# Waits that other waits imply are dropped, and transposed keys get three fixed buffers: a decode attention kernel on one core

## Chip, cores, metric

One core of one Trainium2 chip. The metric is the device time of one execution in microseconds, median of several; most executions agree within 0.1%. The profiler's span is some 1.7 us shorter than the timed execution.

## The reference, cut to what matters

```python
def _A_ref(x, k_cache, v_cache, wq, wo):        # B=4, Sq=1, D=1024, H=32, Sk=8192, Dh=128, bf16
    q = (x @ wq).reshape(B, Sq, H, Dh).transpose(0, 2, 1, 3)
    scores = jnp.einsum("bhqd,bhkd->bhqk", q, k_cache) * (Dh ** -0.5)
    p = _softmax(scores, axis=-1)
    o = jnp.einsum("bhqk,bhkd->bhqd", p, v_cache)
    return o.transpose(0, 2, 1, 3).reshape(B, Sq, H * Dh) @ wo
# ... b: a small gated MLP on the same x; result g*a + (1-g)*b, g = sigmoid of a dot product
```

Keys and values are 2 x 268 MB of the 575.69 MB that must be read. Everything else is small.

## The kernel before

The caches come in pairs of ring slots: four heads of keys (8.39 MB), then four heads of values, alternately. VectorE transposes each key pair in eight pieces of 128x2048 32-bit words, and TensorE multiplies each piece with a sliding window of the query. Values are multiplied as they land.

```python
    ttp = ctx.enter_context(tc.tile_pool(name="ttp", bufs=3))
    # ... manual order on TensorE, VectorE and GpSimd; waits come from the tracking of tiles
    nc.at_finalize(keep_weights)
    nc.at_finalize(begin_early)
    NS = 5
    ring = const.tile([P, NS, RING], BF, name="ring")      # 5 slots of 4.19 MB
    # ...
    def load_pair(src, n, apart=False):
        a = slots(2)
        if a + 1 < NS and not apart:
            nc.sync.dma_start(out=flat[:, lo:lo + 2 * n], in_=src)     # (lo = a * RING)
            return [flat[:, lo:lo + n], flat[:, lo + n:lo + 2 * n]]
        # ... a pair that wraps round the ring: two loads
    # ...
    def k_pair(d):
        # ...
        ks = load_pair(kv_view(A_k_cache, d), RING)
        for n in range(RD):                                # RD = 8
            kn, c = ks[n // JT], n % JT
            T = ttp.tile([P, CJ, 2, 32, 2], BF, name="T", tag="T")
            nc.vector.transpose(out=T[:].rearrange("p j h i e -> p (j h i e)").bitcast(U32),
                                in_=kn[:, c * CJ * Dh:(c + 1) * CJ * Dh].bitcast(U32))
            s = QP - 1 - (RD * t + n)
            for he in range(4):
                half, e = divmod(he, 2)
                for z in range(2):
                    nc.tensor.matmul(sps[:, z, :], lhsT=Z[:, he, s:s + P], rhs=T[:, 16 * z:16 * z + 16, half, :, e],
                                     start=(t == 0 and n == 0 and he == 0),
                                     stop=(t == GD - 1 and n == RD - 1 and he == 3))
```

## Time and profile before

| | before |
|---|---|
| time, median of 3 | 1345.83 us (1345.19 to 1346.19) |
| span in the profile | 1344.2 us, 7958 instructions, 418 of them only wait (EVENT_SEMAPHORE) |
| TensorE / VectorE busy | 77% / 46% |
| transfer queue 1 busy | 99.4% of 16 engines |
| fetches of instructions (queues 8 and 14) | 27 and 7 packets |

A semaphore is a counter by which one engine, or a load, tells another that something is done. In the built programs a transpose carries one wait itself; a further wait stands before it as an instruction of its own, an EVENT_SEMAPHORE. A load is issued when its instruction runs, and has landed when all its data are there. In the lines of profiles, PE is TensorE (PEld its loading of weights), DVE is VectorE, ACT is ScalarE, POOL is GpSimd and SP is SyncE; L375 is line 375 of that run's kernel, and x8 a count.

The end of the chain of work (start, duration, what): the last load of output weights lands at 1340.10, and only four matmuls and a copy follow it.

```profile
1325.25 14.85 DMA ring<-in_A_wo_dram
1340.10 0.04 issue
1340.14 1.04 PE acc L212 x4
...
1341.20 0.57 ACT res L522
```

### The profile page before, as it was taken

The page shows a single profiled execution, that of the slowest core. Times are in us where ns is not written, and L with a number is a line of the kernel's source. Part 1 is how long each engine was busy: PE and PEld are TensorE (multiplying, and loading weights), DVE is VectorE, ACT ScalarE, POOL GpSimd, SP SyncE. Part 2 cuts the span into 40 slices and gives each one's busy share as a digit, 9 for nine tenths or more (in the row PEclk, how much of TensorE's full clock was granted, in tenths as well). Part 3 has the DMA queues.
Part 4 walks back from the last instruction along what each step waited for, and adds up shares of the span by engine and source line. Part 5 has one row for each costly group of instructions (what it writes and reads, how often), then busy time and mean ns, then how long its engine had stood idle before and what let it go on. Part 6 is the DMA issues. An engine that isn't in the chain of part 4 may idle for free.

```text
span 1344.2 us, 7958 instructions
## 1 busy us (share of the span) xinstructions
PE 1034.7 (77%) x4536; PEld 226.7 (17%) x2348; DVE 611.8 (46%) x358; ACT 50.6 (4%) x46; POOL 55.4 (4%) x90
## 2 busy tenths in 40 slices
PE   2665877777788787778987779598778678876898
PEld 0111111111111121111211112111111112111221
DVE  1555655544345554336455556146555244556000
ACT  0000100001000010001000010000100010000100
POOL 2000010001000010001000010000100010000100
PEclk9787988988998888899888889898889799889799
DMA  9999999999999999999999999999999999999997
GB/s 414 437 430 429 440 428 428 444 433 418 446 430 426 432 435 432 438 429 432 430 435 433 437 435 424 431 430 435 433 425 441 431 426 442 431 424 427 434 424 313
DMA packets 14174, 576.19 MB, mean 429 GB/s; under 512 B 1582, under 2 KB 1590, under 8 KB 2108
## 3 DMA queue, kind: packets, MB, share of 16 engines
q1 hardware_dynamic: 14132, 575.69, 99.4%
q8 instruction: 27, 0.44, 0.1%
q14 instruction: 7, 0.06, 0.0%
q10 hardware_dynamic: 8, 0.00, 0.0%
HBM read 575.68 MB, written 0.01 MB: 428 GB/s over the span
## 4 chain that ended last, share of the span: by engine, by line
DMA 66%; PE 13%; DVE 11%; issue 9%; ACT 0%; another core or an unknown queue 0%; DVEq 0%; SPq 0%
DMA ring<-in_A_k_cache_dram 53%; PE o_ps L455 11%; DVE T L375 11%; DMA ring<-in_A_v_cache_dram 9%; DMA ring<-in_B_w_gate_dram 3%; PE S_ps L381 2%; DMA ring<-in_A_wo_dram 1%; ACT PB L426 0%; PE small L475 0%; PE acc L246 0%; DVEq L375 0%; ACT OS L467 0%; PE acc L212 0%; ACT res L522 0%
## 5 line engine op out<-in xcount | busy, mean ns | idle before, releaser
L375 DVE STREAM_TRANSPOSE T<-ring 128x2048 uint32<-128x2048 uint32 x256 | 566.6, 2277 | 494.9 <-DMA ring<-in_A_k_cache_dram 483.5
L381 PE MATMUL S_ps<-T,Z 128*128 128x512 bf16 x2048 | 520.2, 409 | 220.8 <-DVE T L375 220.3
L455 PE MATMUL o_ps<-ring,PB 128*32 128x512 bf16 x2048 | 462.2, 389 | 51.8 <-DMA ring<-in_A_v_cache_dram 47.2
L381 PEld LDWEIGHTS <-Z 128*128 128x128 bf16 x1024 | 105.8, 103 | 630.8 <-issue 623.6
L455 PEld LDWEIGHTS <-PB 128*32 128x32 bf16 x1024 | 101.0, 99 | 409.5 <-issue 368.3
L468 DVE SCALAR_TENSOR_TENSOR OS<-o_ps,mE,OS 128x512 f32<-128x512 f32 x8 | 6.0, 750 | 102.4 <-ACT OS L467 102.4
L406 ACT ACTIVATE PTs<-S_ps,negm 128x1024 bf16<-128x1024 f32 x8 | 8.9, 1114 | 965.3 <-DVE negm L403 965.2
L358 POOL TENSOR_TENSOR Z<-qa,mq 128x16 bf16<-128x16 bf16 x32 | 9.1, 286 | 744.7 <-PE S_ps L381 659.6
L428 POOL COPY PB<-PT 32x1024 bf16<-32x1024 bf16 x16 | 30.5, 1904 | 81.4 <-PE o_ps L455 81.0
L426 ACT COPY PB<-PT 32x1024 bf16<-32x1024 bf16 x16 | 30.6, 1911 | 1.5 <-DVE PT L408 1.4
L309 DVE CAST LT<-small 128x64 bf16<-128x64 f32 x2 | 0.5, 225 | 40.8 <-PE small L307 40.8
L159 PE MATMUL small<-identb,x 6*128 6x6 bf16 x8 | 0.6, 197 | 23.1 <-DMA x<-in_gate_w_dram 23.1
L399 POOL PARTITION_ALL_REDUCE gmx<-mex x8 | 3.2, 397 | 341.3 <-DVE mex L396 341.3
L394 DVE TENSOR_REDUCE m<-S_ps 128x1 f32<-128x1024 f32 x8 | 9.8, 1226 | 15.9 <-PE S_ps L381 15.9
L212 PE MATMUL acc<-ring,LT 128*4 128x512 bf16 x64 | 14.9, 378 | 1.9 <-DMA ring<-in_A_wo_dram 1.1
L408 DVE STREAM_TRANSPOSE PT<-PTs 128x1024 bf16<-128x1024 bf16 x8 | 10.0, 1246 | 12.1 <-ACT PTs L406 12.1
L212 PE MATMUL acc<-ring,hT 128*4 128x512 bf16 x56 | 12.2, 379 | 0.0
L467 ACT ACTIVATE OS<-o_ps,mE 128x512 f32<-128x512 f32 x8 | 5.5, 687 | 157.4 <-PE o_ps L455 157.4
L475 PEld LDWEIGHTS small<-selg,OS 128*128 128x128 f32 x64 | 9.0, 208 | 4.1 <-issue 3.9
L475 PE MATMUL small<-selg,OS 128*128 128x16 f32 x64 | 8.7, 269 | 0.0
L246 PE MATMUL o_ps<-ring,xw 128*4 128x512 bf16 x56 | 5.5, 519 | 3.5 <-DMA ring<-in_B_w_gate_dram 3.5
L246 PE MATMUL S_ps<-ring,xw 128*4 128x512 bf16 x64 | 6.4, 590 | 0.3 <-DVE xw L161 0.3
(71 smaller groups left out, 63.9 us busy)
## 6 DMA issues: line engine op xcount, KB each, us to landing
ring<-in_A_k_cache_dram SPq DMA_DIRECT2D x14, 4096.0 KB
ring<-in_A_v_cache_dram SPq DMA_DIRECT2D x14, 4096.0 KB, 31.3
ring<-in_B_w_gate_dram SPq DMA_DIRECT2D x1, 7168.0 KB, 37.9
ring<-in_B_w_up_dram SPq DMA_DIRECT2D x1, 7168.0 KB, 39.2
ring<-in_B_w_down_dram SPq DMA_DIRECT2D x2, 3584.0 KB, 27.8
ring<-in_A_wo_dram SPq DMA_DIRECT2D x6, 1024.0 KB, 21.0
ring<-in_A_v_cache_dram SPq DMA_DIRECT2D x2, 2048.0 KB, 25.7
ring<-in_A_v_cache_dram SPq DMA_DIRECT2D x4, 1024.0 KB, 24.6
```

Of the source, the lines that this page charges most:

```text
L212: nc.tensor.matmul(out_ap, lhsT=lhsT, rhs=rhs, start=start, stop=True, skip_group_check=True)
L246: nc.tensor.matmul(ps[32 * k:32 * k + Bn, z, :], lhsT=xT[TW * half + t], rhs=cols(w, t, 4 * z + k), start=(half + t == 0), stop=(half == 1 ...
L358: nc.gpsimd.tensor_tensor(out=Z[:, :, QP - 1:QP - 1 + P].rearrange("p e (q c) -> p e q c", c=QP)[:, :, :, 0], in0=qa[:, :, h0:h0 + NQ, b], ...
L375: nc.vector.transpose(out=T[:].rearrange("p j h i e -> p (j h i e)").bitcast(U32), in_=kn[:, c * CJ * Dh:(c + 1) * CJ * Dh].bitcast(U32))
L381: nc.tensor.matmul(sps[:, z, :], lhsT=Z[:, he, s:s + P], rhs=T[:, 16 * z:16 * z + 16, half, :, e], start=(t == 0 and n == 0 and he == 0), ...
L394: nc.vector.tensor_reduce(out=m1[:], in_=sps[:].rearrange("p z n -> p (z n)"), axis=AX.X, op=ALU.max)
L406: nc.scalar.activation(out=PTs[:], in_=sps[:].rearrange("p z n -> p (z n)"), func=ACT.Exp, bias=negm[:, 0:1], scale=scale, accum_out=rs[:, ...
L408: nc.vector.transpose(out=PT[:].rearrange("p j i -> p (j i)"), in_=PTs[:])
L426: nc.scalar.copy(out=Bv[at, :, :, q, :], in_=Pv[at])
L428: nc.gpsimd.tensor_copy(out=Bv[at, :, :, q, :], in_=Pv[at])
L455: nc.tensor.matmul(o_ps[row:row + NM, e, :], lhsT=PB[:, RD * t + c, z, w].rearrange("p e s j -> p (e s j)"), rhs=vn[:, j0 * Dh:(j0 + 4) * ...
L475: nc.tensor.matmul(oT[:, :], lhsT=o_sb[:, q * Dh:(q + 1) * Dh], rhs=selg[:, q].rearrange("p t s -> p (t s)"), start=(q == 0), stop=(q == 3))
```

## The change

When the program is finalised, all engines' instructions are replayed in an order that their semaphores allow. Each engine keeps a clock of what it knows from its waits; a wait is dropped if the engine, or the instruction's other waits, already imply it. The pool for transposed keys gives way to three constant buffers, used in turn. The intent is fewer semaphore instructions and no releases of pool tiles.

```diff
+def drop_implied(nc):
+    # ... streams: the instructions of each engine; known[e]: what engine e has seen
+                        keep = [w for w in waits if not seen(known[e], w)]
+                        for w in list(keep):
+                            k = dict(known[e])
+                            for o in keep:
+                                if o is not w:
+                                    learn(k, o)
+                            if seen(k, w):
+                                keep.remove(w)
+    # ... learn the waits, record the clock at each update, put in the instructions with fewer waits
-    ttp = ctx.enter_context(tc.tile_pool(name="ttp", bufs=3))
+    nc.at_finalize(drop_implied)
+    TB = [const.tile([P, CJ * P], BF, name=f"TB{i}") for i in range(3)]
+    tb_turn = [0]
+    def turned(rows, n, dtype=BF):
+        t = TB[tb_turn[0] % 3]
+        tb_turn[0] += 1
+        return t[0:rows, 0:n] if dtype == BF else t[0:rows, 0:2 * n].bitcast(dtype)
-            T = ttp.tile([P, CJ, 2, 32, 2], BF, name="T", tag="T")
-            nc.vector.transpose(out=T[:].rearrange("p j h i e -> p (j h i e)").bitcast(U32),
+            flat_t = turned(P, CJ * P)
+            T = flat_t.rearrange("p (j h i e) -> p j h i e", j=CJ, h=2, e=2)
+            nc.vector.transpose(out=flat_t.bitcast(U32),
# ... the other users of that pool (gate weights, queries, hidden values, output) take turned(...) as well
```

More of the change, by code (lines that the diff above doesn't have):

```diff
@@ L1 @@
+import copy
 from contextlib import ExitStack
@@ L36, in keep_weights, with seen, learn @@
             block.instructions = kept
+def drop_implied(nc):
+    for f in nc.m.functions:
+        for block in f.blocks[1:2]:
+            streams, at = {}, {}
+            for i in block.instructions:
+                streams.setdefault(i.engine, []).append(i)
+            known = {e: {} for e in streams}
+            level, reached = {}, {}
+            at = {e: 0 for e in streams}
+            def seen(k, w):
+                return k.get(w.id, 0) >= w.wait_value
+            def learn(k, w):
+                for v, clock in reached[w.id]:
+                    if v >= w.wait_value:
+                        for n, x in clock.items():
+                            k[n] = max(k.get(n, 0), x)
+                        break
+                k[w.id] = max(k.get(w.id, 0), w.wait_value)
+            moved, plan = True, []
+            while moved:
+                moved = False
+                for e, todo in streams.items():
+                    while at[e] < len(todo):
+                        i = todo[at[e]]
+                        y = i.sync_info
+                        waits = list(y.on_wait) if y is not None else []
+                        if any(w.wait_mode != "sem-ge-imm" or level.get(w.id, 0) < w.wait_value for w in waits):
+                            break
+                        keep = [w for w in waits if not seen(known[e], w)]
[6 more added lines that the diff above has]
+                                keep.remove(w)
+                        for w in waits:
+                            learn(known[e], w)
+                        if len(keep) < len(waits):
+                            plan.append((i, keep))
+                        for u in (y.on_update if y is not None else []):
+                            level[u.id] = level.get(u.id, 0) + u.update_value
+                            reached.setdefault(u.id, []).append((level[u.id], {**known[e], u.id: level[u.id]}))
+                        at[e] += 1
+                        moved = True
+            if all(at[e] == len(todo) for e, todo in streams.items()):
+                less = {i.name: copy.replace(i, sync_info=mybir.SyncInfo(on_wait=keep, on_update=list(i.sync_info.on_update)))
+                        for i, keep in plan}
+                block.instructions = [less.get(i.name, i) for i in block.instructions]
@@ L218, in gates @@
         rg_ps = small([P, 2, Bn])
-        wrep = ttp.tile([P, 2, DT, P], BF, name="wrep", tag="T")
+        wrep = turned(P, 2 * DT * P).rearrange("p (i t c) -> p i t c", i=2, t=DT)
         for i in range(2):
@@ L229, in add_x @@
     def add_x():
-        xf = ttp.tile([Bn, D], F32, name="xf", tag="T")
-        nc.vector.tensor_copy(out=xf[:], in_=x6[0:Bn])
+        xf = turned(Bn, D, F32)
+        nc.vector.tensor_copy(out=xf, in_=x6[0:Bn])
         for n in range(NH):
@@ L252, in q_done @@
     def q_done():
-        qs = ttp.tile([P, 2, 4, P], BF, name="qs", tag="T")
-        nc.vector.tensor_copy(out=qs[:].rearrange("p z c d -> p z (c d)"), in_=q_ps[:])
+        qs = turned(P, 8 * P).rearrange("p (z c d) -> p z c d", z=2, c=4)
+        nc.vector.tensor_copy(out=qs.rearrange("p z c d -> p z (c d)"), in_=q_ps[:])
         qt = small([P, 2, 4, 4, 32], BF)
@@ L276, in h_done @@
     def h_done():
-        h = ttp.tile([P, 2, 512], F32, name="h", tag="T")
-        nc.scalar.activation(out=h[:], in_=o_ps[:], func=ACT.Silu)
-        nc.vector.tensor_tensor(out=h[:], in0=h[:], in1=acc4[:], op=ALU.mult)
+        h = turned(P, 1024, F32).rearrange("p (z n) -> p z n", z=2)
+        nc.scalar.activation(out=h, in_=o_ps[:], func=ACT.Silu)
+        nc.vector.tensor_tensor(out=h, in0=h, in1=acc4[:], op=ALU.mult)
         for z in range(2):
@@ L518 @@
         use()
-    res = ttp.tile([Bn, D], BF, name="res", tag="T")
+    res = turned(Bn, D)
     nc.vector.tensor_copy(out=res[:, 0:NB], in_=acc[:, 0:NB])
```

## The prediction

> **What bounds the kernel now.** I read the page first, looking for whatever has no idle time. Each digit is a tenth of a slice of 33.6 us; the last row is what the transfer engines moved.
>
> ```profile
> span 1344.2 us, 7958 instructions
> ...
> PE   2665877777788787778987779598778678876898
> ...
> DVE  1555655544345554336455556146555244556000
> ...
> DMA  9999999999999999999999999999999999999997
> GB/s 414 437 430 429 440 428 428 444 433 418 446 430 426 432 435 432 438 429 432 430 435 433 437 435 424 431 430 435 433 425 441 431 426 442 431 424 427 434 424 313
> ...
> q1 hardware_dynamic: 14132, 575.69, 99.4%
> ```
>
> TensorE is busy 77% and VectorE 46%. The 16 DMA engines are busy 99.4% of the span, with no slice under nine tenths but the last. So the kernel is one long read of 575.69 MB. The second view is the table by stretches: middle, then the end in two.
>
> ```profile
> 60.00:1320.00 1260.00, 993.73 (x4258) 216.61 (x2175) 593.07 (x333) 47.91 (x42) 45.07 (x62) 0.90 1.00 432
> ...
> 1330.00:1340.00 10.00, 9.11 (x58) 2.44 (x40) 0.48 (x2) 0.00 (x0) 0.00 (x0) 1.00 0.60 242
> 1340.00:1344.20 4.20, 1.02 (x4) 0.08 (x1) 0.68 (x1) 0.57 (x1) 0.00 (x0) 0.97 0.01 2
> ```
>
> The last two columns are DMA share and GB/s. From 60 to 1320 us the share is 1.00 at 432 GB/s; only the last 14 us are not full. The third question is whether busy transfers hide a late issue, that is, how much work is queued when a load is issued. The chain of work shows one period:
>
> ```profile
> 529.02 2.28 DVE T L375
> ...
> 531.32 29.65 DMA ring<-in_A_k_cache_dram
> ...
> 561.00 0.05 DVEq L375
> ...
> 561.26 2.07 issue
> ...
> 567.72 2.28 DVE T L375
> ...
> 570.01 29.68 DMA ring<-in_A_k_cache_dram
> ```
>
> A key load is issued when the fourth transpose frees half a pair (531.32, 570.01) and lands 29.65 us later. A pair is 4 heads x 8192 x 128 x 2 bytes = 8.39 MB, so 19.4 us at 432 GB/s. The other 29.65 - 19.4 = 10.2 us it stands behind the value load issued before it. So this issue could come about 10 us later, or any amount earlier, and the engines would still not run dry. The chain's "DMA 66%, DVE 11%" looks like a loop through VectorE, but it counts the time in the queue as travel: the period, 570.01 - 531.32 = 38.7 us, is simply two pairs, 2 x 19.4 = 38.8 us of transfer.
>
> **What the Trainium skill says.** "DMA: Bandwidth & Descriptors", section "Where 436 GB/s comes from", gives 435.2 GB/s for the 16 ports into SBUF, and about 358 GB/s as the HBM limit of one core, which it says binds HBM loads. This trace disagrees with the second: 432 GB/s was measured, and the measurement decides. It agrees with the first, 0.7% under it. As an estimate from that page, 575.69 MB / 435.2 GB/s = 1322.8 us is the least that the bytes can take; 2% off the present time would be 0.98 x 1345.83 = 1318.9 us, below it. "Perfetto Trace Analysis", section "Identifying Dependency Chains", says that an instruction waiting on several engines may get EventSemaphore instructions in front of it for the further conditions. This trace agrees: the view of the transpose's line has nearly one for each of the 256 transposes. "VectorE: DVE Perf Modes", section "The DRAIN you can't avoid", reports that eight copies took the same time with a semaphore after each as with one after the last. That concerns increments, but it points the same way: the transposes here follow one another at 17.68 us / 8 = 2.21 us although one lasts 2.27 us, so the extra wait opens no gap.
>
> ```profile
> L375 DVE STREAM_TRANSPOSE T<-ring x256: 2253/2269/2315, 49.9 to 1229.7; 128x2048 uint32<-128x2048 uint32 x128
> L375 DVEq EVENT_SEMAPHORE  x252: 21/21/15795, 52.2 to 1225.4; - x126
> ```
>
> (21 ns is the median; the 15.8 us is time blocked in such a wait, not work.)
>
> **The change part by part.**
> 1. Transposed keys in three fixed buffers in place of a pool of three. Same size (8 KB a partition each), same order of use, same instructions. No byte of DMA and no operation is added. What goes is the pool's release of a buffer, which I take to be why nearly every transpose has a second wait. Cost or gain in work: zero.
> 2. Implied waits dropped. Most of the 252 waits before transposes should go: the transpose three earlier on the same engine is implied by the TensorE wait (those matmuls waited for it), and the landing of a pair is seen once. Also most of the 57 + 17 on the load lines of the SyncE queue, since "VectorE has read the slot" implies "its load has landed"; and a few tens elsewhere. Work removed: 252 x 21 ns = 5.3 us on VectorE's sequencer, beside transposes that keep the engine full, and about 74 x 17 to 28 ns = 1.3 to 2.1 us on SyncE's, which mostly waits. On the path that sets the end in the middle: 0, since an earlier issue only lengthens a queue already 10 us deep.
> 3. First transpose after a landing. It starts about 0.1 us after the data (561.00 to 561.10), 0.05 us of it the extra wait. Over 32 pairs that is 1.6 us at most, if it were on the path; with 10 us queued it is not. I count 0.
> 4. Head. The first load is issued at 0.00 us without waiting. Saving 0.
> 5. Tail. The last weights land at 1340.10, four matmuls take 1.04, the copy 0.57, then the output goes and the program closes at 1344.2. There are one 17 ns wait before the second store and seven of 17 to 28 ns on SyncE in the closing: at most 0.017 + 7 x 0.028 = 0.2 us, of which I count half, 0.1 us. The last weight load has an extra wait too (17 ns, at 1325.2), but is issued 14.85 us before it lands, behind other data.
> 6. Instruction fetch: 27 packets, 0.44 MB, 0.1% of the DMA time. About 350 fewer of 7958 instructions is 4% of 0.1%, some 0.06 us.
>
> Sum: 0.1 + 0.06 = about 0.2 us, inside the spread of the three runs before (1345.19 to 1346.19). I choose 1345.6.
>
> **The rivals.**
> - VectorE or TensorE sets the rhythm and the waits are on it. For it: the chain names the transposes for 11% and "issue" for 9%, and TensorE waits 220 us in total for transposes. The 1.6 us of step 3, plus perhaps 2 us on SyncE, would make 1342 to 1343 us. Against it: DMA share 1.00 over 1260 us. VectorE also waits 483.5 us for key loads; the engine that waits for the transfers does not limit them.
> - Loads issued earlier give the engines a fuller queue and a better rate. The most is 432 to 435.2 GB/s, 0.7%, so 1336 us. For it: the slices vary from 418 to 446. Against it: slices above 435 must be an artefact of how bytes are booked, and they alternate with low ones; the queue is never empty, so a deeper one shows the engines nothing new.
> - A new dependency takes the place of the pool's. Fixed buffers are ordered by overlap of regions, and the odd users (gate weights, queries, hidden values, the output) share them; a coarser order could make a transpose wait for a wrong reader. If a whole group of matmuls (15 us) were added to each of 32 key pairs, the 10 us queue would run dry by up to 5 us a pair: 160 us, about 1500 us. Against it: TensorE goes in order and the rotation is the same, so the last reader of a buffer is the same matmul. I give it 1%.
> - The order of issue on SyncE and ScalarE, which the program does not fix by hand, comes out otherwise. A changed order in the last 20 us could cost or save 1 to 3 us, since there the DMA share falls to 0.60. This widens the range.
>
> **Range and chances.** The spread of repeats is 1.0 us; tail order and chip add 1 to 2 us either way: 1343.0 to 1347.5. Faster by over 2% would beat the port estimate: 0.5%. Slower by over 2% needs a starved queue: 1%. Within 2%: 98.5%.
>
> **What would show it.** Right: DMA share 1.00 and 431 to 433 GB/s from 60 to 1320 us, key loads still landing about 30 us after issue, EVENT_SEMAPHORE at the transposes down from 252 to under 70, transposes still 2.27 us each, last weights landing at 1340 within 1 us. Step 2 wrong: the count stays near 252 (then the waits were not implied). Step 3 wrong, and the first rival right: the whole shortens by 1.5 us or more at the same GB/s. The whole wrong: a middle slice of the DMA row under nine tenths, or issue to landing near 19.4 us, an empty queue.

## More of the kernel before

The page's two queues for instructions, with packets, MB and share of 16 engines:

```profile
q8 instruction: 27, 0.44, 0.1%
q14 instruction: 7, 0.06, 0.0%
```

## The result, and the profile after

Ratios here are the mean time of one kernel's fast runs over the mean of the other's fast runs of the same rounds, so not quite the ratio of the medians quoted.

| | before | after |
|---|---|---|
| time, median | 1346.01 us (4 runs, 1345.19 to 1346.39) | 1344.20 us (4 runs, 1344.16 to 1344.51) |
| ratio | | 0.9988, 95% interval 0.9971 to 1.0005 |
| span | 1344.2 us | 1342.8 us |
| instructions that only wait | 418 (VectorE 259, SyncE 93, GpSimd 31) | 81 (34, 17, 15) |

(Where a text written beforehand says 82, it counts a clearing of semaphores on GpSimd, which is not a wait.)

The predicted 1345.6 us (1343.0 to 1347.5) holds. Yet the four runs of each kernel do not overlap, and 1.4 us of span is more than the 0.2 us of my sum. First the lines of the page after:

```profile
span 1342.8 us, 7621 instructions
...
DMA  9999999999999999999999999999999999999997
...
q1 hardware_dynamic: 14132, 575.69, 99.5%
q8 instruction: 27, 0.44, 0.1%
q14 instruction: 5, 0.04, 0.0%
```

337 instructions are gone and the transfer engines are as full as before. The table by stretches answers to the one of before: same share, same 432 GB/s from 60 to 1320 us.

```profile
60.00:1320.00 1260.00, 994.79 (x4267) 216.47 (x2178) 593.50 (x333) 46.57 (x41) 45.04 (x62) 0.89 1.00 432
1330.00:1340.00 10.00, 8.79 (x53) 1.77 (x33) 0.49 (x2) 0.05 (x1) 0.00 (x0) 1.00 0.58 236
```

The view of the transpose's line (durations in ns: least, median, most) shows 30 waits where 252 were, and no duration changed; the chain of work still has a key load of nearly 30 us, so the queue is as deep as before.

```profile
L443 DVE STREAM_TRANSPOSE TB<-ring x256: 2254/2270/2315, 49.7 to 1227.8; 128x2048 uint32<-128x2048 uint32 x128
L443 DVEq EVENT_SEMAPHORE  x30: 21/21/21, 59.4 to 1221.1; - x30
```

```profile
530.44 29.77 DMA ring<-in_A_k_cache_dram
...
560.30 17.67 DVE TB L443 x8
...
1323.81 15.04 DMA ring<-in_A_wo_dram
1338.85 0.04 issue
1338.89 1.04 PE acc L279 x4
...
1339.95 0.57 ACT TB L590
```

So where does 1.4 us come from? The closing, from the last landing to the end, shrank from 1344.2 - 1340.10 = 4.1 us to 1342.8 - 1338.85 = 3.95 us: 0.15 us. The other 1.25 us is the landing of the last weights, 1340.10 against 1338.85.

Adding up all transfer packets of the traces shows something odd: the bytes moved by any moment up to 1320 us agree within what 0.3 us moves. The transfers as a whole are not faster. But a load counts as landed when the last of the 16 engines has done its part, and these do not finish together: in the last 10 us of the kernel before their share falls to 0.60, and the trace of before ends with one engine alone on the last eight packets of 4 KB, until 1339.64. In the changed kernel the last packet ends at 1338.43.

What else uses these engines? The instructions. Queue 14 brings 8 KB packets, one whenever VectorE has run about 128 more instructions of 64 bytes: in the trace of before the VectorE count stands at 64, 193, 319, 448 and 577 at five of the seven; the remaining two go with other streams, by the counts GpSimd (66) and SyncE (79). After, VectorE's counts at a fetch are 59, 190 and 321: three in place of five. A 64 KB data packet takes 2.42 us, and the one next to a VectorE fetch takes 0.5 to 0.7 us longer. Two fetches fewer, 0.6 us each, would be 1.2 us on one engine. That is theory F (fetches): VectorE's fetched instructions cost one transfer engine time, and every load waits for the slowest engine. Theory A is that of the prediction: only the closing can shorten, the rest is chance. Theory W is that the waiting itself cost the time.

### The profile page after: what moved, and what is told of

Same layout as the page of the kernel before. It is cut to its first block, busy times and chain, and to the rows that moved or that the text cites. A ratio compares the mean times of both kernels' runs of the same rounds, so it can differ in the third digit from the quotient of the medians.

```text
span 1342.8 us, 7621 instructions
## 1 busy us (share of the span) xinstructions
PE 1033.8 (77%) x4536; PEld 226.1 (17%) x2348; DVE 612.4 (46%) x358; ACT 50.6 (4%) x46; POOL 55.3 (4%) x90
## 4 chain that ended last, share of the span: by engine, by line
DMA 65%; DVE 20%; PE 12%; another core or an unknown queue 1%; ACT 0%; issue 0%; SPq 0%; DVEq 0%
DMA ring<-in_A_k_cache_dram 56%; DVE TB L443 20%; PE o_ps L523 10%; DMA ring<-in_A_v_cache_dram 7%; DMA x<-in_gate_w_dram 2%; DMA ring<-in_A_wo_dram 1%; PE S_ps L449 1%; ACT PB L494 0%; PE S_ps L313 0%; PE acc L313 0%; PE small L543 0%; ACT OS L535 0%; PE acc L279 0%; DVE OS L536 0%
## 5 line engine op out<-in xcount | busy, mean ns | idle before, releaser
L443 DVE STREAM_TRANSPOSE TB<-ring 128x2048 uint32<-128x2048 uint32 x256 | 567.3, 2278 | 495.2 <-DMA ring<-in_A_k_cache_dram 493.9
L449 PE MATMUL S_ps<-TB,Z 128*128 128x512 bf16 x2048 | 520.0, 409 | 218.7 <-DVE TB L443 218.5
```

The lines of the kernel that those rows point to most:

```text
L443: nc.vector.transpose(out=flat_t.bitcast(U32), in_=kn[:, c * CJ * Dh:(c + 1) * CJ * Dh].bitcast(U32))
```

## The experiments

The first four separate the parts and give a control; the next four add instructions that wait for nothing; the last four test the queue that hides delays. Times are medians; "kernel before" is the median of nine runs on the same chip in the same rounds.

### The control, the change again, and each part alone

Edits: none; none; and, from the changed kernel and the kernel before:

```diff
# e3_fixed_only: from the changed kernel
-    nc.at_finalize(drop_implied)
# e4_drop_only: from the kernel before
+    nc.at_finalize(drop_implied)
```

> The kernel before, unchanged, timed against itself: the control for the 1.8 us between the medians (1346.01 and 1344.20). Theory A (transfers bound it, only the closing microseconds can shorten): ratio 1.000 within 0.0005, and a second profile whose landing times wander against the first by 0.5 to 1.5 us, as those of the changed kernel do. Rival B (the waits cost a real microsecond in the body): the control is tight, within 0.3 us of the first profile at the landing of the last weights (1340.10 us), so that the 1.25 us by which the changed kernel lands earlier is not chance.

> The changed kernel, unchanged. Theory A: 0.9995 to 0.9999 of the kernel before, that is 0.1 to 0.7 us less (about 0.15 us of the closing, the rest chance). Rival B: 0.9985 to 0.9991, that is 1.2 to 2 us less, with an interval that leaves 1 out.

> Fixed buffers for the transposed keys alone, no wait dropped. Theory A: equal to the kernel before within 0.3 us, and the extra wait instructions before the transposes fall from 252 to well under that, since I put the second wait down to the pool's release. Rival B, buffers: carries most of the 1.2 to 2 us. Rival C: the count stays near 252, because the second wait is a wait for the load or for the engine itself, and it is the dropping that removes it.

> Implied waits dropped, with the pool of three buffers kept. Theory A: equal to the changed kernel within 0.3 us; extra wait instructions in all about 80 as in the changed kernel (82), if implied waits include the pool's. Rival B, waits: carries the 1.2 to 2 us alone. If the pool's release hides the order from the dropping, the count stays well above 82.

Measured, kernel before 1346.09 us:

| run | time us (5 runs) | ratio, 95% interval | instructions that only wait | queue 14 packets | last weights landed |
|---|---|---|---|---|---|
| e1_before_again | 1345.58 (1345.12 to 1345.78) | 0.9997, 0.9984 to 1.0011 | 418 | 7 | 1339.94 |
| e3_fixed_only | 1345.68 (1345.22 to 1346.34) | 1.0000, 0.9987 to 1.0012 | 418 | 7 | 1339.41 |
| e2_after_again | 1344.26 (1344.03 to 1344.61) | 0.9989, 0.9976 to 1.0001 | 81 | 5 | 1338.88 |
| e4_drop_only | 1344.43 (1344.21 to 1344.49) | 0.9989, 0.9977 to 1.0002 | 81 | 5 | 1338.85 |

The rounds' intervals include 1, barely. But all 14 runs with dropped waits lie at 1344.03 to 1344.61, and the ten runs of the control and of the fixed buffers at 1345.12 and above; of the kernel before one run in nine lies lower (1344.74). About 1.3 us is real and belongs to the dropping alone. The landings say the same: 1339.41 to 1340.10 in the three profiles with all waits, 1338.85 to 1338.88 in the three without. Theory A as I wrote it falls: the rest is not chance. The fixed buffers do nothing, and they did not remove the second wait either. The view of the transpose's line in e3_fixed_only:

```profile
L442 DVEq EVENT_SEMAPHORE  x252: 21/21/15893, 52.1 to 1224.7; - x126
```

The built programs say why: nearly every transpose waits for TensorE and for VectorE's own semaphore, that is for the write of the same buffer three transposes earlier, whether the buffer is from a pool or fixed.

### Waits that never block: instructions without waiting

Edit, on top of the changed kernel: before every chosen instruction of one engine, a wait on the first semaphore value that this engine ever waited for.

```diff
+def pad(nc, engine, pick, k):
+    # ... held: the first wait of this engine; for each later instruction that pick() chooses:
+                        for _ in range(k):
+                            out.append(mybir.InstEventSemaphore(name=f"I-{900000 + n}", engine=engine, debug=i.debug, bass_nofuse=True,
+                                                                sync_info=mybir.SyncInfo(on_wait=[held], on_update=[])))
+    nc.at_finalize(lambda nc: pad(nc, mybir.EngineType.DVE, lambda i: isinstance(i, mybir.InstStreamTranspose), 1))
# e6: 4 in place of 1; e7: Pool, InstTensorTensor, 32; e8: PE, InstLdweights, 1
```

> The changed kernel with one wait put back before every stream transpose on VectorE, on a semaphore value that was reached at the very start, so that it never blocks: instructions without waiting. Theory F (fetching VectorE's instructions, 8 KB per 128 of them, takes about 0.6 us each from one of the 16 transfer engines, and every load waits for the slowest of these): VectorE has 264 instructions more, so the fetches in the body (queue 14) go from 5 back to 7, and the time from 1344.2 back to 1345.2 to 1345.8, last weights landing 1.0 to 1.4 us later than in the changed kernel. Rival W (it was the waiting): no blocking wait comes back, so 1344.2 within 0.3.

> Four such waits before every stream transpose on VectorE, 1056 in all. Theory F: 8 more fetches than in the changed kernel, so 8 x 0.6 = about 5 us more: 1347.5 to 1350.5. Rival W: 1344.2 within 0.3, as the transposes still fill VectorE (4 x 21 ns beside 2.2 us each).

> The changed kernel with 1024 waits that never block on GpSimd (32 before each of 32 small multiplications): GpSimd's instruction stream is fetched 8 times more. Theory F with one transfer engine for everybody's instructions: as with VectorE, about 5 us more. Theory F with a transfer engine of its own for each instruction stream: less than that, 0 to 3 us, until that engine becomes the slowest. Rival W: 1344.2 within 0.3.

> The changed kernel with 2271 waits that never block on TensorE, one before every weight load: its stream is fetched about 9 times more, 16 KB each. Theory F with TensorE's fetches on the slowest transfer engine: 9 x 0.5 us = 4 to 6 us more. Theory F with them on another: 0 to 3 us. Rival W: 1344.2 within 0.5 (51 ns each on TensorE's sequencer, about 70 per pair = 3.6 us of a 38.7 us period that has 9 us to spare).

Measured, kernel before 1345.59 us in these rounds; the changed kernel was 1344.26 in its own, on another chip, where the kernel before took 1346.09. So the differences below carry some 0.5 us of doubt:

| run | time us (5 runs) | against 1344.26 | packets on queues 14 / 8 | last weights landed |
|---|---|---|---|---|
| e5_pad_dve_264 | 1345.03 (1344.32 to 1345.43) | +0.8 | 7 / 27 | 1339.64 |
| e6_pad_dve_1056 | 1351.76 (1350.22 to 1352.98) | +7.5 | 13 / 27 | 1347.34 |
| e7_pad_pool_1024 | 1346.13 (1345.99 to 1346.19) | +1.9 | 13 / 27 | 1340.47 |
| e8_pad_pe_2048 | 1346.63 (1345.57 to 1347.12) | +2.4 | 5 / 35 | 1340.27 |

Theory W falls: nothing here blocks, and 1056 instructions on VectorE cost 7.5 us (6.2 us against the kernel before of the same rounds: ratio 1.0042, interval 1.0029 to 1.0056, clear of 1). I had expected 1350.5 at most. Do they delay the transposes instead? No. In e6_pad_dve_1056 eight transposes take what they took in the changed kernel (17.67 us in the chain above); the page and the table by stretches show the transfers suffering:

```profile
563.05 17.66 DVE L462 STREAM_TRANSPOSE TB<-ring 128x2048 uint32<-128x2048 uint32 x8 [21.10 <-DMA ring<-in_A_k_cache_dram]
```

```profile
q1 hardware_dynamic: 14132, 575.69, 99.0%
...
q14 instruction: 13, 0.11, 0.0%
```

```profile
60.00:800.00 740.00, 566.84 (x2427) 121.63 (x1235) 370.00 (x210) 29.79 (x26) 28.25 (x39) 0.89 1.00 432
800.00:1320.00 520.00, 416.59 (x1803) 92.73 (x925) 223.02 (x124) 16.79 (x15) 16.78 (x23) 0.90 1.00 428
```

The second stretch gives way (428 GB/s, against 431 in the changed kernel run again). I read this as: one engine falls behind step by step, the other 15 run ahead on what is queued, and when their lead has used up the queue they too lose time. The landing times of single engines, below, show the first half of that; the second half is argued.

The steps can be seen at single fetches. Take the landing times of e5_pad_dve_264 minus those of the changed kernel (e2_after_again), and the times of the fetches on queue 14:

| between the landings at | fetch in only one of them | difference before and after it |
|---|---|---|
| 337 and 346 us | e5 at 338.2 | +0.43 to +1.51 |
| 813 and 852 us | e5 at 837.7 | +0.89 to +1.85 |
| 1007 and 1066 us | e2 at 1030.6 | +1.40 to +0.69 |
| 1066 and 1115 us | e5 at 1109.6 | +0.69 to +1.42 |

At each of these fetches the landings move by 0.7 to 1.1 us. The steps do not simply add up: with no fetch in one run alone, the difference falls from 1.51 to 0.79 between 346 and 619 us, and in the first 200 us, left out here, it also rises by 0.82 (152 to 171 us) without one. Two executions of the changed kernel differ by up to 0.7 us early on, but by at most 0.23 from 560 us on. For e6, (1347.34 - 1338.88) / 8 fetches = 1.06 us each; I had expected 0.6. The stretching of the neighbouring packet (0.6 to 0.7 us there, where one is found) does not account for the rest, which stays open.

As many fetches for GpSimd (8 more) cost +1.9 us in all, and 8 more of TensorE's 16 KB +2.4 us. So it matters whose instructions they are. The trace does not name the engine that carried a packet. But it keeps sixteen landing times for every load, which I read as one for each transfer engine's part. For the last load of weights, sorted:

| run | last part | the one before it | first part |
|---|---|---|---|
| before | 1340.10 | 1338.62 | 1332.30 |
| after | 1338.85 | 1338.66 | 1332.23 |
| e5_pad_dve_264 | 1339.64 | 1338.66 | 1332.35 |
| e6_pad_dve_1056 | 1347.34 | 1340.49 | 1338.24 |
| e7_pad_pool_1024 | 1340.47 | 1338.88 | 1332.82 |
| e8_pad_pe_2048 | 1340.27 | 1339.95 | 1332.25 |

From the kernel before to the changed kernel the last part comes 1.25 us earlier, the one before it 0.04 us later: the gain in landing lies on one engine alone. It is the one that carries VectorE's instructions: against e2_after_again the landings of the kernel before rise by 0.95 to 1.0 us at VectorE's fetches at 373.2, 638.0, 917.6 and 1190.1, and do not rise at GpSimd's (264.9) and SyncE's (599.6). In e6_pad_dve_1056 the last part falls ever further behind the next: 1.4 us in the load that lands at 249 us in the kernel before, 3.2 at 503, 5.1 at 891, 7.0 at 1320.

In e7_pad_pool_1024 another engine must be the last one. Against e2_after_again its landings rise by 0.4 to 0.7 us at eight of GpSimd's nine fetches (from 105.3 to 1107.2 us; the first, at 24.6, is within the early wander). At VectorE's three (140.1, 605.2 and 1033.8) they do not move: there the difference falls by 0.7 to 1.0, because e2_after_again has its own VectorE fetches at 139.1, 603.4 and 1030.6. So the two streams load different engines. In e8_pad_pe_2048 no engine stands alone, and eight parts land after 1338.2 us where the changed kernel has four: TensorE's fetches seem to be spread over several engines.

E5 brought back 0.8 of the 1.3 us, with as many fetches as the kernel before (five of VectorE either way). That is below the 1.0 us and the 1345.2 us that I had expected at least. Its last landing, 1339.64, lies among the three of the kernels with all waits; the rest of the time may be the doubt of 0.5 us between chips or runs, or the moments of the fetches, and stays open.

### Is it the queue that hides delays?

Edits: `NS = 4` in place of `NS = 5` in each kernel; and a useless operation ahead of every key transpose of the changed kernel:

```diff
# e9_ring4_before, e10_ring4_after
-    NS = 5
+    NS = 4
# e11_dve_work_small (once, 512 wide), e12_dve_work_large (twice, 1024 wide)
+                nc.vector.tensor_reduce(out=idle[:, at:at + 1], in_=mask[:, 0:1].to_broadcast([P, 512]), axis=AX.X, op=ALU.max)
```

> The kernel before with a ring of 4 slots in place of 5. A load is now issued only when the load two before it is wholly used (all eight transposes, 17.7 us after landing) while the one between takes 19.4 us: some 2 us stay queued in place of 10. If the 10 us queue is what hides the waits (my prediction's step), this kernel is slower: 1355 to 1430 us, with a DMA share below 1.00. If the queue doesn't matter: 1346.

> The same 4 slots with the change. With an almost empty queue the waits lie on the path: theory says 2 to 5 us less than the kernel before with 4 slots (about 1 us of instruction fetches, and up to 0.05 to 0.1 us for each of 32 key pairs), against 1.3 us with 5 slots. If the waits cost nothing even there: 1.0 to 1.5 us less, the fetches alone.

> The changed kernel with a useless reduction of some 0.6 us before every key transpose on VectorE: the fourth transpose of a pair ends about 1.8 us later and the eighth about 4.2 us later, less than the 10 us queue. Queue theory with fetches: no cost of the delay itself; 256 more instructions are 2 fetches, so 1345.0 to 1346.0, as with the 264 waits (1345.03). If VectorE were on the path: 32 x 1.8 to 4.2 us more, 1400 us and over.

> Two useless reductions of some 1.1 us before every key transpose: the eighth ends about 16 us later, more than the queue holds for the value loads (31.3 - 19.4 = 11.9 us), while VectorE stays under full load (some 36 of 38.7 us a pair). Queue theory: now the transfer engines run dry, 1400 to 1500 us and a DMA share below 0.97. If only VectorE's busy time counted: 1347 to 1350 (4 more fetches).

Measured, kernel before 1345.73 us:

| run | time us | ratio, 95% interval | DMA share of queue 1 |
|---|---|---|---|
| e9_ring4_before | 1416.20 (5 runs, 1408.84 to 1420.91) | 1.0518, 1.0492 to 1.0545 | 96.2% |
| e10_ring4_after | 1421.75 (4 runs, 1417.34 to 1425.62) | 1.0565, 1.0544 to 1.0586 | 95.3% |
| e11_dve_work_small | 1346.37 (5 runs, 1345.77 to 1348.22) | 1.0010, 0.9997 to 1.0022 | 99.4% |
| e12_dve_work_large | 1563.17 (4 runs, 1556.08 to 1563.92) | 1.1601, 1.1577 to 1.1624 | 86.9% |

The queue is what hides. In e11_dve_work_small the chain of work shows the delay, and that the load takes it back:

```profile
533.01 28.84 DMA ring<-in_A_k_cache_dram
...
561.94 2.31 DVE TB L447
564.25 0.57 DVE idle L446
...
570.39 2.23 DVE TB L447
...
572.64 27.91 DMA ring<-in_A_k_cache_dram
```

From landing (561.85) to the next issue (572.64) it is 10.8 us in place of the 9.0 of before (560.97 to 570.01), 1.8 us more in this pair, with the same work added in all 32, and the load lands after 27.9 us in place of 29.7. Cost in the total: 2.1 us over the changed kernel (again on another chip). Two more VectorE fetches (the page has 7 packets on queue 14) would be 1.4 to 2.2 us of it, an estimate from the steps above. I had expected at most 1346.0; the median missed by 0.4. With delays beyond the queue (e12) the engines run dry, much harder than I thought (1563, not 1400 to 1500): the share in its page falls to

```profile
q1 hardware_dynamic: 14132, 575.69, 86.9%
```

although VectorE is busy only 76% of the span.

E9 came out within its 1355 to 1430. E10 is a miss. With a short queue I expected the dropped waits to save 2 to 5 us, since the waits now lie on the path. The changed kernel came out 5.5 us slower instead. The two sets of runs overlap (1417.34 to 1425.62 against 1408.84 to 1420.91) and each spreads over 8 to 12 us, ten times as much as with five slots, so I read it as: no gain is seen, and whether there is a loss is open.

## Why the prediction was right, and where its steps failed

- **What bounds the kernel** held. 432 GB/s and share 1.00 from 60 to 1320 us in both, a queue some 10 us deep, and delays below that hidden (e11), above it not (e12), a shorter ring slower (e9).
- **Step 1, cost of fixed buffers zero**: right in size (ratio 1.0000), wrong in reason. The second wait before a transpose was VectorE's wait for itself, not the pool's release: 252 with fixed buffers as well.
- **Step 2, waits worth nothing on the path**: right for the waiting. The counts went further than I said (30 before the transposes, where I expected "under 70"; 1 on the load lines, where I expected "most" of 74 to go).
- **Step 3, 0.1 us after each landing is not on the path**: held with five slots; even with four slots no gain was seen. My sign that it was wrong, and the first rival right, was a kernel 1.5 us faster at the same GB/s. That came (1.8 us between the medians, 432 GB/s in both), and it pointed at the wrong cause: waits that never block, put back in e5 and e6, cost time as well, and 1.8 us more on VectorE in each pair (e11) cost 2 us and not 57. The sign did not tell waiting from fetching.
- **Step 4, head**: 0, as said. **Step 5, closing**: 0.15 us measured, 0.1 counted.
- **Step 6, instruction fetch, 0.06 us**: the term that was mis-sized. I took 4% of the fetch traffic's 0.1% share, as if the saving were spread over 16 engines and all instructions. In fact only VectorE's saving removes fetches (five to three; TensorE's 27 stay), the whole of it falls on the one engine that finishes last, and every load waits for that one. The landing came 1.25 us earlier, all of it on that engine, twenty times what I counted; e5, which put the fetches back, returned 0.8 us of it in time and in landing.
- **Landing of the last weights within 1 us of 1340**: 1338.85, so missed by 0.15 us, for the reason of step 6.
- **The rivals**: a VectorE rhythm would have made e11 cost 57 us (32 x 1.8) or more; it cost 2. A better rate from a deeper queue: 432 GB/s in both. A new dependency from fixed buffers: none (e3). Another order of issue: the loads went out in the same order in both traces.

The range held because 1.2 us fits into it, not because the sum was right: 0.2 us were counted, 1.3 us and more came. The mechanism of the gain was not among my four rivals; it stood in step 6, at a twentieth of its size.

## What to carry to other kernels

When a kernel keeps all transfer engines full, a wait that is dropped saves no waiting; first measure how much work is queued at each issue: here a delay of 1.8 us in every pair, with some 10 us queued, was hidden (but for 2.1 us in all, which its fetches can account for), and one beyond the queue was not (e12). Where a profile says 99% for 16 engines together, ask which single one ends last (a load's sixteen landing times tell how far it lags) and what else it carries: here a few kilobytes of fetched instructions, 0.1% of the traffic on average, cost about 1 us for every 128 instructions of VectorE (e6), so instructions that do nothing are not free even on an engine that is busy for less than half of the span. And run the kernel before against itself: without the control, 1.3 us of 1345 would have been taken for chance.

## What the Trainium skill lacked or had wrong

- "DMA: Bandwidth & Descriptors", section "Where 436 GB/s comes from", says that HBM binds loads at about 358 GB/s for a core: 432 GB/s were measured over 1260 us, with one core running, 0.7% under the port figure of 435.2.
- "Advanced Engine Details and Errata", section "ISA Cache", gives instruction cache lines of 16 KB, 256 instructions, and I had not drawn on it. The trace agrees for TensorE (27 fetches of 16 KB); VectorE's, GpSimd's and SyncE's came in 8 KB, for VectorE one per 128 instructions (counts 64, 193, 319, 448, 577). The section calls the size configurable per engine, so this need not be an error of the page.
- What a fetch of instructions during the run costs a kernel that fills the transfer engines stands on no page as a figure; it belongs to "Runtime: NRT & Kernel Launch", section "Instruction fetch mechanics". Here landings moved by 0.7 to 1.1 us per fetch of VectorE's stream, and the whole by less for as many of GpSimd's (+1.9 us for 8). Nor does a page say that the streams of VectorE and GpSimd load different transfer engines (e7).
- "VectorE: DVE Perf Modes", section "The DRAIN you can't avoid", finds for eight copies that a semaphore after each costs no extra time. That holds for VectorE's own pace here (17.66 us for eight transposes with 32 extra waits, 17.67 without), and the page says nothing of the rest of the kernel: +7.5 us for 1056 such instructions.
